# Keys and squares moved to TensorE, inversion steps in halves, and a new order of all steps in a delta-rule attention + MLP-mixer kernel

## The chip, the core and the metric

The kernel runs on one core of a Trainium2 chip. Its engines are TensorE (PE, matmuls; PEld, its weight loads), VectorE (DVE), ScalarE (ACT), GpSimd (POOL) and SyncE (SP, which issues the DMAs). The metric is device time in microseconds; the time before is 624.92 us, the median of 3 runs (623.73 to 625.54).

## The reference

```python
# q, k, v: (4, 8, 768, 48), beta: (4, 8, 768)
k_n = k / (np.linalg.norm(k, axis=-1, keepdims=True) + 1e-06)
for t in range(S):                                   # 768 steps
    y[:, :, t] = einsum('bhd,bhde->bhe', q[:, :, t], state)
    v_old = einsum('bhde,bhd->bhe', state, kt)
    state = state + bt * einsum('bhd,bhe->bhde', kt, vt - v_old)
x = y.transpose(0, 2, 1, 3).reshape(B, S, H * D)     # (4, 768, 384)
h = relu(x.T @ w_tok1) @ w_tok2                      # token mixing, 768 -> 256 -> 768
u = x + h.T
out = u + relu(u @ w_ch1) @ w_ch2                    # channel mixing, 384 -> 1536 -> 384
```

## The kernel before

The 768 steps of a batch are cut into 6 units of 128 steps, 24 units over the four batches; a unit holds two chunks of 64 steps for all 8 heads. All arithmetic is fp32. Jobs, each a Python generator, issue the work, and one long string, `order`, says how often each job is advanced and in what order. Every engine runs its own instructions in that order and waits only for what it needs; the string is thus the schedule, and nothing else sets the order. Job names are a letter and a number:

- `k` loads a unit's keys and queries, `v` its values, `w` loads and rounds a piece of a weight matrix (two ScalarE activations L286/L287, a VectorE shift L289, a GpSimd add L293).
- `p` prepares a unit (function `prep`). The squares of the keys are summed and turned into norms and scales `cs`; keys and queries are transposed by TensorE (`p_t`) and copied by ScalarE into `kq` (L566, L587); the mask times `cs` (`mb`, L574) and the keys times `cs` (L592) are made by VectorE for units 0 to 3 and by GpSimd behind them. Units 12 and up are transposed by VectorE instead.
- `c` and `d` (from unit 12 on, `c` alone) make the gram matrices of the two chunks: matmuls into `p_g` (L511), then a VectorE product with `mb` into `gm` (L517).
- `t` gathers the triangular blocks of a unit, `i` inverts those of a round of units (round 0: units 0 to 3, round 1: 4 and 5, then four at a time), `f` puts the inverse back. In rounds 0 and 1 the blocks go by copies (L674, L677, L679) into a tile `r2`, are transposed by VectorE (L731), inverted as 16x16 blocks in 14 steps of a product and an addition (L747, L751), transposed and scaled for TensorE (L757, L758, L759), and transposed back (L764). From round 2 on they go through DRAM and take 30 steps.
- `h` and `j` join the inverted blocks with matmuls (`p_z`, `p_x`, L781, L794, L855) and ScalarE copies (L785, L799, L873).
- `r` is one step of the recurrence over a chunk: `p_k` (L924), a VectorE subtraction (L931), `p_w` and `p_y` (L948, L944), a ScalarE copy (L954), `p_s` and `p_y` (L962, L963), the new state (L971). Steps r0 to r11 belong to batch 0.
- `m0` and `m1` are the mixers of batches 0 and 1; `p` L1597, `p_h` L1612 and `p_c` L1672 are their matmuls. m0 needs the steps r0 to r11. `T`, `A`, `F` and `B` are the mixers of batches 2 and 3, in forms with fewer multiplications.
- `x`, `z` and `Y` issue matmuls on zeros into a tile `p_warm` of their own; they fill idle time of TensorE.

In units 0 to 3 the keys come from the padded load by four ScalarE copies each:

```python
for cc in range(2 if u < RU else 0):
    for par in range(2):
        nc.scalar.copy(kst[PAR[par ^ cc], :, cc], heads[PAR[cc], :, par, 0:D])
```

## Time and profile before

| | |
|---|---|
| median of 3 runs | 624.92 us (623.73 to 625.54) |
| the profiled execution | 626.48 us, span 624.7 us |
| mean granted TensorE clock | 0.973 |
| busy in the span | PE 594.3 us, DVE 466.1, ACT 256.6, POOL 110.2 |

A profile is of one execution. The span runs from its first to its last instruction; its time is 1.8 us more. Busy shares are means over stages with different limits, so the stages are read one by one: the row of a window gives its start and end, its length, and the busy time and instruction count of each engine, then the granted clock of TensorE (1.00 is full), the share of the DMA engines and GB/s. A line of the timeline gives start, duration, engine, line, operation, output and input, and in brackets the idle time ahead and what ended it.

### The profile page before, as it was taken

How to read it: one execution, taken by the hardware profiler on the slowest of the kernel's cores; microseconds unless marked ns; L12 is line 12 of the kernel's file. 1: busy time of each engine (PE TensorE's matmuls, PEld its weight loads, DVE VectorE, ACT ScalarE, POOL GpSimd, SP SyncE). 2: the span in 40 equal slices, each digit the busy share in tenths (PEclk: the TensorE clock that was granted, in tenths of full speed). 3: DMA queues.
4: the chain of work that ended last, by engine and by line, in shares of the span. 5: the costliest groups of instructions: out<-in, count | busy, mean ns of one | idle time of the engine just before them, and what ended most of it. 6: DMA issues, size and time to landing. Idle time of an engine off the chain costs nothing.

```text
span 624.7 us, 20909 instructions
## 1 busy us (share of the span) xinstructions
PE 594.3 (95%) x8733; PEld 519.7 (83%) x8733; DVE 466.1 (75%) x1160; ACT 256.6 (41%) x682; POOL 110.2 (18%) x150
## 2 busy tenths in 40 slices
PE   8489898899999999999999999999999999999998
PEld 5467776667898988977888888896699999999997
DVE  4986876986889845697567986866688898675874
ACT  7748787448522344213551305423252241404200
POOL 2346355215311121003020130011000000000000
PEclk9978897999999999999999999998999999999999
DMA  9566567657653244554544443134102012020001
GB/s 220 125 140 146 143 151 192 137 139 177 129 113 71 64 103 91 102 116 96 104 74 123 93 88 76 35 80 120 32 2 39 1 17 48 14 52 13 14 26 50
DMA packets 154605, 55.52 MB, mean 89 GB/s; under 512 B 129648, under 2 KB 148976, under 8 KB 154512
## 3 DMA queue, kind: packets, MB, share of 16 engines
q1 hardware_dynamic: 154512, 54.20, 38.3%
q8 instruction: 68, 1.11, 0.8%
q14 instruction: 25, 0.20, 0.1%
HBM read 41.19 MB, written 11.21 MB: 84 GB/s over the span
## 4 chain that ended last, share of the span: by engine, by line
PE 74%; DVE 10%; DMA 4%; ACT 3%; issue 2%; SPq 2%; POOL 0%; ACTq 0%; DVEq 0%
PE p_c L1672 13%; PE p_r L1502 13%; PE p_o L1693 10%; PE p_a L1574 6%; PE p_b L1574 6%; PE p_g L511 3%; PE p_h L1612 3%; DVE x L751 2%; PE p L1597 2%; DVE sub L747 2%; PE p_k L924 1%; DMA x<-n_dram 1%; PE p_h L1242 1%; PE p_s L962 1%; PE p_y L1038 1%
## 5 line engine op out<-in xcount | busy, mean ns | idle before, releaser
L1672 PE MATMUL p_c<-u_t,wc 128*128 128x256 f32 x432 | 101.6, 386 | 0.6 <-issue 0.6
L1672 PEld LDWEIGHTS p_c<-u_t,wc 128*128 128x128 f32 x432 | 79.6, 190 | 11.9 <-issue 1.1
L1693 PE MATMUL p_o<-wc,r 128*128 128x192 f32 x360 | 64.6, 331 | 0.7 <-DVE xb L1632 0.7
L751 DVE TENSOR_TENSOR x<-x,sub 128x84 f32<-128x84 f32 (+24 forms) x178 | 59.6, 335 | 6.1
L747 DVE TENSOR_TENSOR sub<-x 128x84 f32<-128x84 f32 (+24 forms) x178 | 57.7, 324 | 8.1 <-DMA x<-n_dram 3.5
L1693 PEld LDWEIGHTS p_o<-wc,r 128*128 128x128 f32 x360 | 58.4, 190 | 2.3 <-DVE xb L1632 1.3
L1681 ACT ACTIVATE r<-p_c 128x512 f32<-128x512 f32 x36 | 21.5, 596 | 49.3 <-PE p_c L1672 43.9
L511 PE MATMUL p_g<-kq 48*64 48x128 f32 (+1 forms) x704 | 35.2, 288 | 3.0 <-ACT kq L587 3.0
L517 DVE TENSOR_TENSOR gm<-p_g,mb 128x512 f32<-128x512 f32 x44 | 28.9, 684 | 9.5 <-PE p_g L511 8.4
L484 POOL TENSOR_TENSOR v_st<-v_st,nrm 128x384 f32<-128x384 f32 x12 | 11.2, 931 | 132.4 <-DMA v_st<-in_v_dram 104.8
L511 PEld LDWEIGHTS p_g<-kq 48*64 48x64 f32 (+1 forms) x704 | 27.1, 141 | 7.9 <-ACT kq L587 4.0
L574 POOL TENSOR_TENSOR mb<-mask_c,cs 128x512 f32<-128x512 f32 x20 | 21.2, 1061 | 65.3 <-DVE cs L552 35.7
L293 POOL TENSOR_TENSOR wc<-w_f,d 128x384 uint32<-128x384 uint32 x24 | 24.6, 1030 | 43.3 <-DVE w_f L289 20.2
L1502 PE MATMUL p_r<-t_d,wc 128*128 128x192 f32 x160 | 28.8, 326 | 0.0
L1515 DVE TENSOR_TENSOR kq<-kq,p_r 128x384 f32<-128x384 f32 x40 | 21.1, 552 | 10.2 <-PE p_r L1502 8.3
L1515 DVE TENSOR_TENSOR gm<-gm,p_r 128x384 f32<-128x384 f32 x40 | 21.2, 552 | 8.1 <-PE p_r L1502 5.8
L400 DVE STREAM_TRANSPOSE kq<-pads 128x512 f32<-128x512 f32 x24 | 25.6, 1109 | 1.6 <-DMA pads<-in_k_dram 1.2
L1502 PEld LDWEIGHTS p_r<-t_d,wc 128*128 128x128 f32 x160 | 26.5, 190 | 0.0
L1693 PE MATMUL p_o<-wc,s 128*128 128x192 f32 x144 | 25.7, 330 | 0.7 <-DVE xb L1632 0.7
L1502 PE MATMUL p_r<-pads,wc 128*128 128x192 f32 x128 | 25.4, 326 | 0.0
L1693 PEld LDWEIGHTS p_o<-wc,s 128*128 128x128 f32 x144 | 23.3, 190 | 1.3 <-DVE xb L1632 1.0
L1632 DVE TENSOR_TENSOR xb<-xb,p_o 128x192 f32<-128x192 f32 x42 | 14.7, 349 | 12.7 <-PE p_o L1693 12.3
(315 smaller groups left out, 1390.6 us busy)
## 6 DMA issues: line engine op xcount, KB each, us to landing
d<-in_moe_w_ch_dram SPq DMA_DIRECT2D x24, 384.0 KB, 3.9
v_st<-in_v_dram SPq DMA_DIRECT2D x96, 48.0 KB, 2.7
out_dram<-xb SPq DMA_DIRECT2D x23, 192.0 KB, 2.1
kst<-in_k_dram SPq DMA_DIRECT2D x64, 48.0 KB, 2.6
n_dram<-gm SPq DMA_DIRECT2D x72, 32.0 KB, 2.4
pads<-in_k_dram SPq DMA_DIRECT2D x24, 96.0 KB, 3.0
pads<-in_q_dram SPq DMA_DIRECT2D x24, 96.0 KB, 2.7
gm<-w_dram SPq DMA_DIRECT2D x72, 32.0 KB, 2.1
```

The source lines that it names most:

```text
L293: nc.gpsimd.tensor_tensor(out=dst.bitcast(U32), in0=f, in1=lo, op=ALU.add)
L400: nc.vector.transpose(kq_of[p // 2][:, i, :, p % 2].rearrange("f p (s g) -> f p g s", g=G), rows_of[i].rearrange("s p (g d) -> s p g d", g ...
L511: nc.tensor.matmul(p_g[PAR[i ^ cc ^ swap(u)], p], kqt[f, p, cc, 0], kqt[f, p, cc])
L517: nc.vector.tensor_tensor(out=blocks(gm_of(u))[:, :, cc, D:GW].rearrange("s p (two n) -> s p two n", two=2), in0=p_g, in1=made[u][:, :, cc ...
L747: nc.vector.tensor_tensor(out=tmp, in0=by[0].to_broadcast(list(to.shape)), in1=by[1].to_broadcast(list(to.shape)), op=ALU.mult,)
L751: nc.vector.tensor_tensor(out=to, in0=to, in1=tmp, op=ALU.add)
L1502: nc.tensor.matmul(p[:, i], pieces[q // width][:, at : at + 128], f[f"u{n}"], start=first and i == 0, stop=True, skip_group_check=True,)
L1515: nc.vector.tensor_tensor(out=o, in0=o, in1=p, op=op_of(sign))
L1574: nc.tensor.matmul(p, a[:, i], w[:, i // 2, i % 2], start=first and i == 0, stop=True, skip_group_check=True,)
L1672: nc.tensor.matmul(p_c[:, k], piece_of(wc1, cb, f * 128)[:, f * 128 : (f + 1) * 128], u_t[:, cb], start=(cb == 0), stop=(cb == NCB - 1),)
L1681: nc.scalar.activation(r2[:, m], p_c, ACTF.Relu)
L1693: nc.tensor.matmul(p, a[:, m], wc2[:, m, j], start=(start and i == 0), stop=(i == NM - 1), skip_group_check=True,)
```

## The change

1. Squares. For units 0 to 11, `prep` now transposes the keys first, ScalarE squares the transposed keys out of PSUM, and TensorE sums the squares over the 48 features with a matmul on a column of ones, 16 for a unit, into 8 columns of `p_warm`; ScalarE takes the norms from there. The VectorE reduction is left out. The zero matmuls write 120 columns where they wrote 128.
2. Keys. For units 0 to 3, the ScalarE copies are left out; four matmuls on a piece of the identity put the keys into PSUM (`p_m`), and VectorE scales them from there.
3. Inversion. Each step's product and addition are issued in two halves (two products, then two additions), by 16x16 block in rounds 0 and 1 and by row from round 2 on.
4. The string `order` is another one.

```diff
-        nc.scalar.square(ksq, kst.rearrange("s p c d -> s (p c) d"))
-        nc.vector.tensor_reduce(out=ksum, in_=ksq, axis=mybir.AxisListType.X, op=ALU.add)
-        nc.scalar.sqrt(nrm_f, ksum)
...
+        p_t = turn(kp, True)                       # u < 12
+        yield
+        nc.scalar.square(ksq, p_t)
+        yield
+        for p in range(NP):
+            for cc in range(2):
+                for i in range(2):
+                    at = 2 * p + cc
+                    nc.tensor.matmul(
+                        p_n[PAR[i ^ cc], at : at + 1], ksq[:, p, cc], pair[:, i : i + 1]
+                    )
+        yield
+        norms(p_n, ksum)
+        yield
+        nc.scalar.copy(kqt[:, :, :, 0], p_t)
...
+        if u < RU:
+            keys = ps_seq([128, NP, 2, D], "p_m")
+            for cc in range(2):
+                for par in range(2):
+                    nc.tensor.matmul(
+                        keys[PAR[par ^ cc], :, cc], ident[:, PAR[cc]],
+                        heads[:, :, par, 0:D],
+                    )
+        scaler.tensor_tensor(out=keys_out, in0=keys, in1=wide(cs), op=ALU.mult)
...
-            nc.vector.tensor_tensor(
-                out=tmp, in0=by[0].to_broadcast(list(to.shape)),
-                in1=by[1].to_broadcast(list(to.shape)), op=ALU.mult,
-            )
-            nc.vector.tensor_tensor(out=to, in0=to, in1=tmp, op=ALU.add)
+            for to, half, by in zip(tos, tmps, bys):
+                nc.vector.tensor_tensor(
+                    out=half, in0=by[0].to_broadcast(list(to.shape)),
+                    in1=by[1].to_broadcast(list(to.shape)), op=ALU.mult,
+                )
+            for to, half in zip(tos, tmps):
+                nc.vector.tensor_tensor(out=to, in0=to, in1=half, op=ALU.add)
...
-    w10 x*4 z w10*2 z w1*4 k1*3 z k1*3 z b p1 z p1 k0*6 p0*2 b*2 p1 w2 p0*5 p1*2
+    w17 z w17*3 z x*2 w3*2 b z*3 k0*2 k1 w18 b*2 w3 k1 p1 w3 k2 p1 x p0 x*2 k3*2
```

In the changed file the lines are others: the squares' matmuls are L621, the key moves L646, the halves L814 and L819, and what was L562/L582, L511, L517, L731, L757, L758, L759, L764 is L576, L518, L524, L790, L825, L826, L827, L832.

TensorE at the first units, before. `p_t` are transposes (L562 of keys, L582 of queries), `pads` and `lent` hold the loaded rows, `p_g` grams, `p_warm` zeros:

```order
L562 MATMUL p_t<-ident,pads 128x128 x8
L582 MATMUL p_t<-ident,pads 128x128 x4
L235 MATMUL p_warm<-warm 128x512
L511 MATMUL p_g<-wc_120 64x128 x16
L582 MATMUL p_t<-ident,pads 128x128 x4
L511 MATMUL p_g<-wc_120 64x128 x16
L562 MATMUL p_t<-ident,lent 128x128 x4
L582 MATMUL p_t<-ident,lent 128x128 x4
L511 MATMUL p_g<-kq 64x128 x10
```

The same place in the changed kernel:

```order
L576 MATMUL p_t<-ident,pads 128x128 x4
L245 MATMUL p_warm<-warm 128x120
L576 MATMUL p_t<-ident,pads 128x128 x4
L245 MATMUL p_warm<-warm 128x120 x2
L621 MATMUL p_warm<-marks,ksq 64x1 x32
L576 MATMUL p_t<-ident,pads 128x128 x4
L646 MATMUL p_m<-pads,ident 64x4x48 x4
L518 MATMUL p_g<-wc_124 64x128 x16
L576 MATMUL p_t<-ident,lent 128x128 x4
L576 MATMUL p_t<-ident,pads 128x128 x4
L518 MATMUL p_g<-wc_124 64x128 x16
```

The squares of two units and one unit's key move now stand between the first transposes and the first grams.

VectorE at the end of i0, before (`x` holds the blocks, `r_124` is `r2`, `gm<-p_g` the gram products of unit 4):

```order
L751 TENSOR_TENSOR x<-x,sub 128x2x2x13
L289 TENSOR_SCALAR w_f<-d_403 128x384
L747 TENSOR_TENSOR sub<-x 128x28
L751 TENSOR_TENSOR x<-x,sub 128x2x14
L753 MEMSET x 128x32
L755 MEMSET x 128x16x16
L757 STREAM_TRANSPOSE r_124<-x 128x512
L759 TENSOR_SCALAR r_124<-r_124,even 128x512
L517 TENSOR_TENSOR gm<-p_g,mb 128x4x128 x2
L542 TENSOR_REDUCE ksum<-ksq 128x8
L764 STREAM_TRANSPOSE r_124<-x 128x1024
```

The same place in the changed kernel:

```order
L819 TENSOR_TENSOR x<-x,sub 128x2x13 x2
L524 TENSOR_TENSOR gm<-p_g,mb 128x4x128
L814 TENSOR_TENSOR sub<-x 128x14 x2
L819 TENSOR_TENSOR x<-x,sub 128x14 x2
L821 MEMSET x 128x32
L823 MEMSET x 128x16x16
L825 STREAM_TRANSPOSE r_128<-x 128x512
L827 TENSOR_SCALAR r_128<-r_128,even 128x512
L832 STREAM_TRANSPOSE r_128<-x 128x1024
L524 TENSOR_TENSOR gm<-p_g,mb 128x4x128
```

One gram product moved ahead of the last step, the other behind the back transpose, and the reduction is gone from between.

ScalarE behind i0, before (`z_571<-p_z` and `wc_120<-p_x` belong to the joins of units 0 and 1, `kq<-p_t` and `ksq` to the preparation of units 4 to 6, `d` to weights):

```order
L758 ACTIVATE r_124<-r_124,odd 128x512
L539 ACTIVATE ksq<-kst_99 128x384
L674 COPY r_124<-gm 128x8x32
L547 ACTIVATE nrm<-ksum 128x8
L548 ACTIVATE ksum<-nrm,eps 128x8
L785 ACTIVATE z_571<-p_z,sides 128x8x16 x2
L286 ACTIVATE d_609<-d_609 128x384
L287 ACTIVATE d_609<-d_609 128x384
L785 ACTIVATE z_571<-p_z,sides 128x8x16 x2
L697 ACTIVATE wc_120<-r_124,even 128x8x32 x2
L785 ACTIVATE z_571<-p_z,sides 128x8x16 x2
L566 COPY kq<-p_t 128x4x128
```

The same place in the changed kernel:

```order
L826 ACTIVATE r_128<-r_128,odd 128x512
L299 ACTIVATE d_704<-d_704 128x384
L300 ACTIVATE d_704<-d_704 128x384
L756 ACTIVATE wc_124<-r_128,even 128x8x32
L853 ACTIVATE z_712<-p_z,sides 128x8x16 x4
L756 ACTIVATE wc_124<-r_128,even 128x8x32
L853 ACTIVATE z_712<-p_z,sides 128x8x16 x2
L756 ACTIVATE gm<-r_128,even 128x8x32
L867 COPY wc_124<-p_x 16x8x16 x7
L941 COPY zst<-p_z 32x256 x2
```

The squares, norms and copies of later units no longer stand between the joins there.

318 lines of the change are left out of this document (184 added, 134 removed).

## The prediction

> **What bounds the kernel now.** I read the page first (busy shares, slices, the chain that ended last), then the windows, then the timelines of VectorE, TensorE and ScalarE ahead of 140 us.
>
> ```profile
> span 624.7 us, 20909 instructions
> PE 594.3 (95%) x8733; PEld 519.7 (83%) x8733; DVE 466.1 (75%) x1160; ACT 256.6 (41%) x682; POOL 110.2 (18%) x150
> PE   8489898899999999999999999999999999999998
> PEclk9978897999999999999999999998999999999999
> PE 74%; DVE 10%; DMA 4%; ACT 3%; issue 2%; SPq 2%; POOL 0%; ACTq 0%; DVEq 0%
> ```
>
> TensorE is the bound, except in the first eight or nine slices. The windows (length, then busy time of PE, PEld, DVE, ACT, POOL, then the granted clock) follow the program's stages: up to the first inversion (i0, 27.4 us), to its first use (h0, 41.5), to the first recurrence step (r0, 54.7), to r8 (101), to the stretch in which the mixer takes over, and the rest.
>
> ```profile
> 8.00:27.40 19.40, 14.06 (x230) 10.87 (x228) 15.24 (x38) 17.15 (x47) 4.05 (x6) 1.00 0.67 152
> 27.40:41.50 14.10, 7.67 (x44) 4.39 (x45) 12.35 (x36) 4.51 (x9) 6.45 (x6) 0.76 0.81 181
> 41.50:54.70 13.20, 12.05 (x287) 10.77 (x288) 9.13 (x16) 10.55 (x29) 7.05 (x10) 0.83 0.53 112
> 54.70:101.00 46.30, 40.71 (x1266) 36.37 (x1264) 35.21 (x92) 39.52 (x108) 25.70 (x33) 0.94 0.66 154
> 101.00:117.00 16.00, 13.50 (x237) 9.85 (x239) 11.15 (x35) 9.38 (x26) 5.53 (x7) 0.68 0.67 168
> 117.00:138.80 21.80, 21.42 (x259) 14.03 (x259) 18.46 (x54) 7.14 (x19) 4.68 (x6) 1.00 0.60 151
> 138.80:430.00 291.20, 287.11 (x5139) 246.97 (x5139) 214.32 (x549) 109.57 (x321) 52.82 (x69) 1.00 0.45 99
> 430.00:624.70 194.70, 190.80 (x1269) 182.31 (x1268) 147.36 (x327) 53.65 (x116) 0.00 (x0) 0.98 0.11 25
> ```
>
> From 117 us on TensorE is idle for 0.4 + 4.1 + 3.9 us only. What is left for it there is the same work in both programs, so faster vector steps after 117 us gain next to nothing, and the new order there has some 8 us to win or add to. The time is decided ahead of that: by when the first mixer's matmuls (m0) can run without a gap. Ahead of i0 ScalarE is the fullest (17.15 of 19.4), VectorE next; during i0 VectorE alone works (12.35 of 14.1); from 41.5 to 101 ScalarE and TensorE share the load.
>
> **Ahead of i0: keys and squares.** Prices for what goes and what comes:
>
> ```profile
> L435 ACT COPY kst<-pads x8: 337/349/352, 5.6 to 8.8; 64x192 f32<-64x192 f32 x8
> L539 ACT ACTIVATE ksq<-kst 128x384 f32<-128x384 f32 x7 | 3.7, 523 | 0.1
> L566 ACT COPY kq<-p_t 128x512 f32<-128x512 f32 x10 | 5.8, 577 | 2.4 <-PE p_t L562 2.3
> L542 DVE TENSOR_REDUCE ksum<-ksq 128x8 f32<-128x384 f32 x12 | 6.5, 545 | 4.7 <-ACT ksq L539 4.6
> 8.70 1.57 PE L257 MATMUL p_b<-pick,b_rows 32*64 32x16 f32 x48
> 10.20 1.09 PE L562 MATMUL p_t<-ident,pads 128*128 128x128 f32 x8
> 451.03 19.67 PE p_r L1502 x120
> ```
>
> Removed from ScalarE: 16 key copies at 0.35 us, 5.6 us. Its square grows from 384 to 512 elements and reads PSUM, as the kq copy does: 0.58 for 0.52, so +0.06 for each of 12 units. Removed from VectorE: 12 reductions at 0.545, 6.5 us, four or five of them ahead of i0. The scaling of units 0 to 3 by L592 now reads PSUM; masks from SBUF (L574) and gram products from PSUM (L517) cost alike there, so nothing is put down for it.
>
> Added to TensorE: the code's 24 beta matmuls are 48 records, so each fp32 matmul runs as two passes. A unit's squares are 16 matmuls, 32 passes, on 64-column weights in alternating column halves with one moving column. No row has this form. Upper end: a 128x128 transpose takes 1.09/8 = 0.136 us, half as many weight columns 0.068, so 2.2 us for a unit. Lower end: half of what the beta matmuls take, 0.5 us. Nearest is that beta row itself (64-column weights, alternating halves, short moving side): 1.57/48 = 0.033, so 1.05 us for a unit, which I take; 12.6 us for 12 units. A unit's key move is 8 passes of 192 columns at 19.67/120 = 0.164: 1.3 us one after the other, 0.65 if the two column halves overlap fully; I take 1.0, 4 us for four. In all TensorE gets 16.6 us more.
>
> The Trainium skill (TensorE: Matmul & The Clock Gate, section LDWEIGHTS) has a weight load last its columns divided by 1.2 GHz, whatever the rows: 53 ns for 64 columns. By it a unit's squares would be 32 x 53 ns = 1.7 us, an estimate, and the beta row with its 33 ns is below it; the sum would lose some 4.6 us on seven units.
>
> Of the added work, the squares of units 0 to 4 and the moves of units 0 to 2 stand ahead of unit 3's last gram: 5 x 1.05 + 3 x 1.0 = 8.3 us. In 8 to 27.4 us TensorE is idle for 5.3 us, and its fillers (two lines of code) take:
>
> ```profile
> 8.00:27.40 19.40, 2.99 (x10) 1.12 (x8) 1.00 0.67 152
> 8.00:27.40 19.40, 0.60 (x8) 0.47 (x8) 1.00 0.67 152
> ```
>
> 5.3 + 3.6 = 8.9 us, less about 0.9 for the fillers that the new order keeps there: room for 8.0. ScalarE and VectorE have slack to give now, but TensorE would be full, and it cannot be quite full: each unit's squares wait for ScalarE's square, and the next unit's grams stand behind them. If a third of its old waits stays (1.8 us), i0 begins 8.3 + 1.8 - 8.0 = **2.0 us later** (range -1 to +6). The norms also move behind the transposes, and the second unit's key lands no earlier (the same loads stand ahead of it in SP's queue, in another order).
>
> **i0 to the first recurrence step.** Within i0, starts tell what an instruction costs:
>
> ```profile
> 32.59 0.28 DVE L747 TENSOR_TENSOR sub<-x 128x112 f32<-128x112 f32 x1
> 32.90 0.28 DVE L751 TENSOR_TENSOR x<-x,sub 128x112 f32<-128x112 f32 x1
> 36.15 0.21 DVE L747 TENSOR_TENSOR sub<-x 128x52 f32<-128x52 f32 x1
> 36.39 0.21 DVE L751 TENSOR_TENSOR x<-x,sub 128x52 f32<-128x52 f32 x1
> 36.52 0.35 DVE L289 TENSOR_SCALAR w_f<-d 128x384 uint32<-128x384 uint32 x1
> 39.40 1.37 DVE L759 TENSOR_SCALAR r<-r,even 128x512 f32<-128x512 f32 x1 [0.79 <-ACT r L758]
> 40.69 1.27 DVE L517 TENSOR_TENSOR gm<-p_g,mb 128x512 f32<-128x512 f32 x2
> 116.10 0.40 DVE L751 TENSOR_TENSOR x<-x,sub 128x228 f32<-128x228 f32 x1
> 116.41 0.35 DVE L971 TENSOR_TENSOR ss_t<-ss_t,p_s 128x192 f32<-128x192 f32 x1
> 41.51 2.21 PE L781 MATMUL p_z<-r,wc 64*64 64x32 f32 x64 [2.06 <-DVE gm L517]
> ```
>
> One that needs the result ahead of it starts 0.31 us after it at 112 elements and 0.24 at 52: about 0.19 us + 1 ns an element. One that doesn't starts 0.13 after 52 elements and 0.31 after 228: about 0.08 + 1 ns. A step of N elements now takes 2 x (0.19 + N). In halves it is four instructions, each needing the one before last: two periods of max(2 x (0.08 + N/2), 0.19 + N/2), N in thousands. Over the 14 steps (28 to 112 elements, 1120 in all): 7.6 us now, 6.8 then, **-0.8 us**. Ends: -3.2 if all gaps vanish (14 x 0.23), +5.3 if an instruction always takes its full 0.19 (14 x 0.38).
>
> Against this stands a rule of the Trainium skill (VectorE: DVE Perf Modes, sections Terms and Rules for kernel authors): after every operation the pipe is flushed before the next issues, so one should minimize the count of operations. By it halves lose 5.3 us here; the L289 that started 0.13 us into a 0.21 us instruction disagrees.
>
> After the steps, the two gram products of unit 4 (40.69) stood between i0 and h0, which waited for them until 41.51. Now one is ahead of the last step and one behind the back transpose, so h0 can follow L759, 40.77 in this trace: 0.7 us earlier, less the 0.6 of the product moved ahead: **-0.1**. The back transpose itself has one product fewer ahead of it: **-0.6**, which the f jobs wait for.
>
> From there to r0 ScalarE is busy for 10.55 of 13.2 us. Two squares (0.52), two kq copies (0.58) and a copy to r2 (0.65) no longer stand between: 2.85 us. Half of it is taken, since the chain there alternates with TensorE: **-1.4 us** (0 to -2.85).
>
> ```profile
> L674 ACT COPY r<-gm 128x256 f32<-128x256 f32 x1 | 0.7, 651 | 2.2 <-DVE gm L517 2.2
> 103.12 3.94 DMA x<-n_dram
> 106.00:110.00 4.00, 4.00 (x11) 2.53 (x10) 2.96 (x13) 2.16 (x7) 0.32 (x1) 0.50 1.05 329
> ```
>
> **r0 to m0's matmuls.** From 54.7 to 101 TensorE gets four units' squares, 4.2 us, into 5.6 us of idle time; ScalarE's work is the same; VectorE loses four or five reductions and gains 0.8 us in i1, which lies on this stretch. I put **-0.4** (range -2 to +3). From 101 on, r9 to r11 run between i2's steps on VectorE (i2's input lands at 107, 103.12 + 3.94): 18 steps at 0.07 saved and two reductions are -2.3 us, against two units' squares, 2.1 us, part of them where TensorE is full: **-1.0** (range -5 to +2).
>
> Behind 138.8 us: 0, by equal work. DMAs, SP's and POOL's instructions are the same in number. In SP's queue weight loads are moved among the key and query loads; one that lands late holds ScalarE's rounding and the kq copies behind it, which is the upper end of i0's range.
>
> **Sum:** 2.0 - 0.8 - 0.1 - 0.6 - 1.4 - 0.4 - 1.0 = **-2.3 us**: a span of 622.4, and 624.2 for this execution, whose own time was 626.5 beside a span of 624.7. Its time lies 1.6 above the median of the runs, 624.92; against that median I predict **622.6 us**.
>
> **Rivals.**
> - The cold stretch goes too. At 106 to 110 the clock was 0.50, after TensorE's waits of 101 to 106, and in 101 to 117 it idled for 2.5 us. With more to do there and i2 begun ahead of r8, it may stay warm: 2.5 idle + about 2 of slowed matmuls back, 618. Against it: TensorE still follows VectorE there.
> - No difference. The relief of ScalarE and VectorE ahead of i0 is worth nothing, since TensorE, full by then, sets i0's start, and r8 onwards follows i2, which waits for DMA round trips as before. Then the -1.4 and -1.0 go, i0's delay is cancelled by the rest: 625.
> - Slower: the squares cost 0.068 a pass, 2.2 us a unit. That is 1.15 more for each: 5.7 ahead of i0 and 2.3 on the last two units, 630.6. It decides from 2.3 / 7 = 0.33 us a unit more, that is 0.043 a pass; the transposes speak for it, the beta row against.
> - Slower: every half pays in full. At 0.19 us + 1 ns an element whatever it depends on, a step costs 0.38 us more: 5.3 in i0, as much in i1, 6.8 in i2's 18 steps, half of it on the chain, and the 2.3 saved in steps lost: 633.5. The two starts inside running instructions speak against it. It is what the rule of the Trainium skill (VectorE: DVE Perf Modes, section Terms) would bring.
>
> **How the numbers follow.** Chances: the forecast 0.33 (its own range 619.5 to 623), the warm stretch 0.13, no difference 0.26, costly squares 0.19, flush 0.04, a new wait elsewhere in the new order 0.05. A measurement of this kernel tells about 0.3% (1.9 us) from no change. Faster by more than that: 0.13 + 0.32 = 0.45; same: 0.26; slower: 0.29, from the last three and a sliver of the forecast. The range, 613 to 632, reaches past the warm stretch and over the costly squares.
>
> **What would show it.** The new matmuls' rows: 1.05 us a unit for the squares, 1.0 for a move. i0's transpose (L731 before) at 29.4 instead of 27.4, with TensorE over 95% busy ahead of it. Its 14 steps in 6.8 us, halves starting inside each other. r0 near 53.8, r8 near 99, the first p_c near 136.5, TensorE's idle time behind it still about 8 us. I am wrong if a unit's squares take over 1.4 us, if i0 starts beyond 32, or if idle time of several us appears behind 140 us.

## The result, and the profile after

The changed kernel takes 663.72 us (median of 4 runs, 660.36 to 670.45), the kernel before 624.33 us (median of 4, 623.58 to 625.54): a ratio of 1.0611, 95% interval 1.0557 to 1.0665. In the run of 670.45 us the chip was in a slower state, and the ratios leave such runs out. The prediction was 622.6 us. The profiled execution took 660.36 us beside a span of 658.6; the spans below are compared with the 624.7 of before.

From the page of the changed kernel, the span and the busy times:

```profile
span 658.6 us, 22031 instructions
PE 614.6 (93%) x9149; PEld 532.5 (81%) x9149; DVE 466.9 (71%) x1497; ACT 252.2 (38%) x666; POOL 109.6 (17%) x150
```

TensorE is busy for 20.3 us more than the 594.3 of before, and idle for 13.6 us more. Where, three windows tell: up to the first p_c, from there to the first matmul of the third mixer, and the rest (columns as above). First before:

```profile
0.00:138.70 138.70, 116.27 (x2330) 90.36 (x2330) 104.44 (x284) 93.32 (x247) 57.26 (x82) 0.90 0.67 156
138.70:422.00 283.30, 279.71 (x4987) 242.11 (x4983) 210.05 (x542) 105.80 (x307) 51.32 (x68) 1.00 0.44 96
422.00:624.70 202.70, 198.30 (x1425) 187.24 (x1421) 151.64 (x335) 57.52 (x131) 1.60 (x1) 0.98 0.14 33
```

and the same windows of the changed kernel:

```profile
0.00:161.20 161.20, 137.41 (x2795) 105.89 (x2795) 100.46 (x392) 90.23 (x232) 59.51 (x83) 0.89 0.63 134
161.20:459.90 298.70, 282.39 (x4968) 242.54 (x4966) 214.68 (x771) 104.16 (x303) 47.16 (x64) 0.99 0.43 93
459.90:658.60 198.70, 194.78 (x1397) 184.06 (x1389) 151.78 (x335) 57.85 (x132) 2.96 (x3) 1.00 0.14 32
```

Two different losses. Ahead of the first p_c 22.5 us: TensorE is busy 21.1 us longer, and its idle time has not shrunk (22.4 us, now 23.8), although ScalarE and VectorE have 3 and 4 us less to do. Behind it 15.4 us, 12.7 of them idle time (3.6 us, now 16.3). The last window gives 4.0 back; its granted clock was 0.98 in the execution before.

The larger part of the first loss lies behind i0. From r1's p_w to the first p_c, before:

```profile
59.50:138.70 79.20, 70.73 (x1632) 55.49 (x1630) 62.59 (x174) 51.80 (x141) 32.35 (x41) 0.91 0.62 153
```

and now:

```profile
66.40:161.20 94.80, 84.32 (x1893) 66.20 (x1891) 63.36 (x259) 54.63 (x142) 34.57 (x41) 0.87 0.57 129
```

15.6 us more, 13.6 of them busy time of TensorE, at a lower clock.

The new matmuls, from the groups by line (count, busy time, mean ns of one, idle time ahead):

```profile
L621 PE MATMUL p_warm<-marks,ksq 128*64 128x1 f32 x384 | 14.0, 202 | 2.3 <-ACT ksq L614 2.3
L646 PE MATMUL p_m<-lent,ident 128*64 128x192 f32 x16 | 1.7, 339 | 0.0
```

The moves out of `pads` take another 1.7 us. 14.0 / 12 = 1.17 us for a unit's squares (0.036 us a pass) and 3.4 / 4 = 0.85 for a move: 17.4 us in all, about the 16.6 put down. The price of the matmuls themselves was right; what was wrong is what their place in the schedule costs.

The first two units on TensorE and ScalarE, from the timeline of the changed kernel:

```profile
10.10 0.66 PE L576 MATMUL p_t<-ident,pads 128*128 128x128 f32 x4
10.79 0.60 ACT L614 ACTIVATE ksq<-p_t 128x512 f32<-128x512 f32 x1
11.78 1.10 PE L621 MATMUL p_warm<-marks,ksq 128*64 128x1 f32 x32
12.99 0.60 ACT L614 ACTIVATE ksq<-p_t 128x512 f32<-128x512 f32 x1 [1.61 <-PE p_warm L621]
13.64 1.10 PE L621 MATMUL p_warm<-marks,ksq 128*64 128x1 f32 x32 [0.77 <-ACT ksq L614]
...
16.32 1.59 PE L518 MATMUL p_g<-wc 64*64 64x128 f32 x32 [0.19 <-ACT wc L638]
...
18.76 0.54 ACT L299 ACTIVATE d<-d 128x384 f32<-128x384 f32 x1 [1.61 <-DMA d<-in_moe_w_ch_dram]
20.29 0.56 ACT L638 COPY wc<-p_t 128x512 f32<-128x512 f32 x1
20.90 1.15 PE L518 MATMUL p_g<-wc 64*64 64x128 f32 x32 [1.97 <-ACT wc L638]
```

The first grams of the kernel before:

```profile
12.60 1.37 PE L511 MATMUL p_g<-wc 64*64 64x128 f32 x32
15.94 1.16 PE L511 MATMUL p_g<-wc 64*64 64x128 f32 x32 [1.38 <-ACT wc L587]
```

Before, ScalarE squared the loaded keys of units 0 and 1 and VectorE summed them at 7 to 10.3 us, while TensorE ran zeros and the beta matmuls; nothing of it stood behind a transpose. Now the transposes come first, at the same 10.1 us, and behind them TensorE and ScalarE take turns: square, sums, next square (it waits until the sums have read `ksq`), sums, norms, copies, grams. The first grams start 3.7 us later. The second ones start 5.0 later, and a weight load has a part in this: ScalarE waited 1.6 us for it at 18.76 and rounded the weights ahead of the copy that these grams need. i0 starts at 35.9 in place of 27.4.

VectorE in i0. A line holds both halves of a step's product (x2); the additions between them are left out:

```profile
38.64 0.32 DVE L814 TENSOR_TENSOR sub<-x 128x44 f32<-128x44 f32 x2
39.12 0.33 DVE L814 TENSOR_TENSOR sub<-x 128x50 f32<-128x50 f32 x2
...
41.90 0.36 DVE L302 TENSOR_SCALAR w_f<-d 128x384 uint32<-128x384 uint32 x1 [1.19 <-ACT d L299]
```

A step of 88 elements in halves takes 39.12 - 38.64 = 0.48 us; the formula of the prediction gives 0.50. But a weight's rounding now stands inside the steps and waits for ScalarE, 1.2 us in which VectorE does nothing.

Behind the first p_c, what TensorE waited for (in all, times, longest), in the changed kernel:

```profile
PE p_k L992 <- DVE ss_t L1039: 3.6, 3, 3.2
PE p_o L1761 <- DVE xb L1700: 2.8, 3, 1.1
PE p_k L1081 <- DVE ss_t L1138: 2.0, 1, 2.0
PE p_z L923 <- DVE t L885: 2.0, 2, 1.0
```

and in the same stretch before, where the longest wait was 0.7:

```profile
PE p_o L1693 <- DVE xb L1632: 1.4, 3, 0.7
```

All of them are waits for VectorE, most for its steps of the recurrence and the joins. The longest, 3.2 us at 265 us, shows what stood in front there. A later unit's keys land late; ScalarE's square waits for them, VectorE's sum waits for the square, and the state (L1039) that TensorE needs stands behind the sum.

```profile
266.89 0.52 ACT L584 ACTIVATE ksq<-kst 128x384 f32<-128x384 f32 x1 [4.61 <-DMA kst<-in_k_dram]
267.44 0.55 DVE L587 TENSOR_REDUCE ksum<-ksq 128x8 f32<-128x384 f32 x1 [4.71 <-ACT ksq L584]
...
268.27 0.32 DVE L1039 TENSOR_TENSOR ss_t<-ss_t,p_s 128x192 f32<-128x192 f32 x1
```

Other waits of this stretch lead back to loads in the same way. Two waits of a join at 351 us (1.2 us together) are for a gram product that stands behind such a sum, three of joins at 239, 324 and 458 us (2.4 together) for a VectorE transpose that waits for its blocks from DRAM, and the 2.0 us of L1081 end behind an inversion whose blocks VectorE had waited 5.2 us for. That is 8.8 of the 16.3 us of idle time. ScalarE's squares waited 29.1 us in all for keys here, and 7.5 before.

### The profile page after: what moved, and what is told of

The parts are those of the page before. It is cut to its first block, busy times and chain, and to the rows that moved or that the text cites. A ratio compares the mean times of both kernels' runs of the same rounds, so it can differ in the third digit from the quotient of the medians.

```text
span 658.6 us, 22031 instructions
## 1 busy us (share of the span) xinstructions
PE 614.6 (93%) x9149; PEld 532.5 (81%) x9149; DVE 466.9 (71%) x1497; ACT 252.2 (38%) x666; POOL 109.6 (17%) x150
## 5 line engine op out<-in xcount | busy, mean ns | idle before, releaser
L1740 PE MATMUL p_c<-u_t,wc 128*128 128x256 f32 x432 | 103.6, 389 | 1.1 <-issue 0.9
L814 DVE TENSOR_TENSOR sub<-x 128x56 f32<-128x56 f32 (+41 forms) x351 | 73.1, 248 | 10.8 <-DMA x<-n_dram 8.8
L819 DVE TENSOR_TENSOR x<-x,sub 128x56 f32<-128x56 f32 (+41 forms) x351 | 71.0, 242 | 0.2
L518 PE MATMUL p_g<-kq 48*64 48x128 f32 (+1 forms) x704 | 35.7, 280 | 8.9 <-ACT kq L638 7.3
L518 PEld LDWEIGHTS p_g<-kq 48*64 48x64 f32 (+1 forms) x704 | 26.9, 136 | 14.3 <-ACT kq L638 8.5
L524 DVE TENSOR_TENSOR gm<-p_g,mb 128x512 f32<-128x512 f32 x44 | 29.0, 683 | 10.8 <-PE p_g L518 10.7
L1761 PE MATMUL p_o<-wc,s 128*128 128x192 f32 x144 | 25.8, 331 | 0.8 <-DVE xb L1700 0.8
L1580 ACT COPY kq<-p_r 128x384 f32<-128x384 f32 x24 | 11.4, 476 | 37.8 <-PE p_r L1570 35.8
L299 ACT ACTIVATE d<-d 128x384 f32<-128x384 f32 (+1 forms) x34 | 18.4, 540 | 17.4 <-DMA d<-in_moe_w_ch_dram 9.0
```

What stands on the lines that cost most here:

```text
L518: nc.tensor.matmul(p_g[PAR[i ^ cc ^ swap(u)], p], kqt[f, p, cc, 0], kqt[f, p, cc])
L524: nc.vector.tensor_tensor(out=blocks(gm_of(u))[:, :, cc, D:GW].rearrange("s p (two n) -> s p two n", two=2), in0=p_g, in1=made[u][:, :, cc ...
L814: nc.vector.tensor_tensor(out=half, in0=by[0].to_broadcast(list(to.shape)), in1=by[1].to_broadcast(list(to.shape)), op=ALU.mult,)
L819: nc.vector.tensor_tensor(out=to, in0=to, in1=half, op=ALU.add)
L1740: nc.tensor.matmul(p_c[:, k], piece_of(wc1, cb, f * 128)[:, f * 128 : (f + 1) * 128], u_t[:, cb], start=(cb == 0), stop=(cb == NCB - 1),)
L1761: nc.tensor.matmul(p, a[:, m], wc2[:, m, j], start=(start and i == 0), stop=(i == NM - 1), skip_group_check=True,)
```

## The experiments

Times are medians; a ratio is to the kernel before on the same chip, with its 95% interval. The rows were measured on several chips, so that small differences are to be read from the ratios. "Old order" is the order of before. Where the code has other steps than that order, a unit's steps stand at its old places, as each expectation says. The expectations also name the theories between which a run is to decide.

| kernel | us | ratio |
|---|---|---|
| halves, old order | 619.53 | 0.9921 (0.9893 to 0.9950) |
| halves in rounds 0 and 1 alone, old order | 619.76 | 0.9969 (0.9931 to 1.0006) |
| halves, three more zero matmuls, old order | 623.32 | 0.9992 (0.9958 to 1.0025) |
| halves + key moves, old order | 622.79 | 0.9972 (0.9937 to 1.0007) |
| halves + key moves, squares of units 0 to 3 (2 of 16 matmuls), old order | 628.96 | 1.0081 (1.0045 to 1.0118) |
| halves + key moves, squares of units 0 to 3, old order | 634.16 | 1.0174 (1.0104 to 1.0243) |
| halves + squares of units 4 to 11 (2 of 16 matmuls), old order | 636.33 | 1.0202 (1.0139 to 1.0266) |
| halves + squares of units 4 to 11, old order | 642.35 | 1.0266 (1.0212 to 1.0320) |
| the same and a zero matmul a unit | 646.53 | 1.0348 (1.0280 to 1.0415) |
| the same, squares out of SBUF | 653.29 | 1.0494 (1.0431 to 1.0557) |
| all edits, old order | 655.85 | 1.0510 (1.0455 to 1.0564) |
| all edits, new order: the changed kernel | 663.72 | 1.0611 (1.0557 to 1.0665) |

The parts add up: halves -0.8%, moves and squares of units 0 to 3 +2.5%, squares of units 4 to 11 +3.5%, together 1.052; all edits in the old order measured 1.051. The new order adds some 1.0% to that; the two intervals just touch, and the traces under experiment 3 tell more.

**1. Halves alone.**

```diff
 # kernel before, inversion steps
-nc.vector.tensor_tensor(out=tmp, ...); nc.vector.tensor_tensor(out=to, ...)
+two products, then two additions, as in the change
```

> The kernel before with one part of the change, the steps of the inversions in two halves; the order and everything else as before. Theory work (the 17.4 us that TensorE is busy longer, 14.0 for squares and 3.4 for key moves, lie on its path wherever they stand): the halves cost nothing, the two early rounds gain about 28 x 0.13 = 3.6 us on VectorE, of which some reaches the end: 620 to 625. Theory order (what is lost is lost to waits of the new order): the same, 620 to 625. Theory halves (twice as many VectorE instructions delay whatever VectorE does between them): 630 or more, with TensorE idle behind 140 us.

619.53 us, 0.9921: a gain of 0.8%, 4.9 us. Theory halves is out. The halves are the one part of the change that pays. Their gain is more than the 2.9 us of the prediction (0.8 in i0, as much in i1, 1.3 in i2).

**2. The changed kernel with whole steps.**

```diff
-            for to, half, by in zip(tos, tmps, bys): ...
+            nc.vector.tensor_tensor(out=tmp, ...); nc.vector.tensor_tensor(out=to, ...)
```

> The changed kernel with the steps of the inversions whole again; squares, key moves and the new order stay. Theories work and order: 663 to 668, since the halves are worth a few us at most. Theory halves: 650 or less, the 13.5 us of TensorE's additional idle time are gone.

664.21 us, 1.0645 (1.0570 to 1.0720). The loss is not the halves'; in the new order their gain does not stand out from the noise.

**3. All edits in the old order.**

```diff
 # order of before
-k0*6 p0*2 b*2 p1 w2 p0*5 p1*2
+k0*2 p0*2 b*2 p1 w2 p0*5 p1*2     # no key copies; p0 to p3 have one step more near their end
```

> The changed kernel's squares, key moves and halves in the order of before. A unit's steps stand at the places where its old steps stood: for units 0 and 1 one for one, for the others transposes and square at the place of the old fourth step, the squares' matmuls at the fifth, norms and copy at the sixth, scales and mask at the seventh; the key move beside the last step or the one before it. Theory work: 17.4 us less what the halves gain and what fits into idle time, 634 to 642. Theory order: 621 to 629, since the additional waits belong to the new order and the early stage has idle time and zero matmuls enough. Below 625 would say that all the loss is the order's.

655.85 us, 1.0510: above what either theory gave. Its windows:

```profile
0.00:171.40 171.40, 147.41 (x2747) 115.25 (x2747) 101.21 (x389) 90.01 (x231) 57.35 (x82) 0.81 0.59 127
171.40:455.10 283.70, 279.52 (x4986) 242.17 (x4982) 214.38 (x776) 106.62 (x310) 51.42 (x68) 1.00 0.44 97
```

The second window, behind the first p_c, is 283.7 us with 4.2 idle, as before: the 15 us there belong to the new order alone. The other traces bear this out. From the first p_c to the start of the last one it is 260.0 to 263.3 us in all thirteen profiled kernels with the old order, and 275.6 to 279.7 in all seven with the new one. Ahead of the first p_c the old order is worse, 171.4 against 161.2, with a granted clock of 0.81. So the new order comes to the first p_c 10 us earlier, and loses more than that behind it. And the edits cost 36 us beside the halves alone, not 17: something more than the matmuls' own time is lost.

**4. Two of sixteen square matmuls, new order.**

```diff
-for p ...: for cc ...: for i ...:
-    nc.tensor.matmul(p_n[PAR[i ^ cc], at : at + 1], ksq[:, p, cc], pair[:, i : i + 1])
+for i in range(2):
+    nc.tensor.matmul(p_n[PAR[i]], ksq[:, 0, 0], pair[:, i : i + 1].to_broadcast([128, NB]))
```

> The changed kernel in its own order with 2 of a unit's 16 square matmuls left, each writing eight columns: the norms come from the sums of one block alone, all other work is as in the changed kernel. It takes 24 x 14/16 and more, some 12 us, off TensorE. Theory work: 650 to 654, the whole 12 us come back. Theory order: 660 or more, since TensorE then waits longer at the same places.

659.60 us, 1.0552 (1.0484 to 1.0620): 4 of the 12 us, and the interval overlaps with that of the changed kernel. i0 stays at 35.8, but not because the sums cost nothing. Unit 0's grams start at 14.03 us, 2.3 earlier than in the changed kernel; then ScalarE waits for the weight load of above, which lands no earlier, and unit 1's grams stand behind it as late as there (the copy L638 is L633 here):

```profile
18.81 0.54 ACT L299 ACTIVATE d<-d 128x384 f32<-128x384 f32 x1 [3.94 <-DMA d<-in_moe_w_ch_dram]
20.96 2.04 PE L518 MATMUL p_g<-wc 64*64 64x128 f32 x32 [4.31 <-ACT wc L633]
```

Behind it the clock was at one half for 7 us of this execution, and at full in the one of the changed kernel. So this run cannot tell what the sums cost in i0; experiment 15 can, in the old order.

**5. Later units' squares, old order.**

```diff
+OLD_SQ = (0, 1, 2, 3)      # prepared as before, with ScalarE's key copies
+# units 4 to 11: squares on TensorE; old places 4: transposes, square; 5: sums; 6: norms, copy; 7: scales, mask
```

> The order of before with the halves and with the squares of units 4 to 11 summed by TensorE; units 0 to 3 are prepared as before, with ScalarE's key copies. Theory chain (the loss ahead of i0 is the longer way to the norms of units 0 to 3: transposes, square, sums, norms one behind the other; the later units' squares are nearly free): 617 to 623, beside 619.5 for the halves alone. Theory later units (each later unit's squares and its longer hold on a PSUM bank delay the joins and the recurrence, 14 us from r0 to m0): 630 to 636.

642.35 us, 1.0266: 23 us above the halves alone, for 8 x 1.17 = 9.4 us of matmuls. The stretch from r1's p_w to the first p_c, first with the halves alone:

```profile
57.80:135.90 78.10, 69.56 (x1629) 54.60 (x1629) 64.02 (x260) 52.25 (x142) 32.58 (x41) 0.93 0.65 158
```

and here:

```profile
62.50:163.50 101.00, 88.51 (x1824) 71.61 (x1818) 61.09 (x254) 53.09 (x141) 32.08 (x40) 0.78 0.51 120
```

TensorE is busy 19.0 us longer, of which 8.6 are squares, and idle for 4.0 more. The rest goes with the clock column, 0.78 against 0.93: the same 192 passes of the grams take 14.9 us in place of 12.1, the 24 passes of m0's first matmul (L1606, here L1718) 11.5 in place of 9.8. (This execution took 646.75 us, the longest of the four.)

**6. Key moves alone, old order.**

```diff
+keys = ps_seq(...)            # first step: four matmuls on pieces of the identity
+nc.scalar.square(ksq, keys)   # out of PSUM; VectorE sums as before
```

> The order of before with the halves and with the keys of units 0 to 3 moved by TensorE, as a unit's first step; ScalarE squares them out of PSUM, VectorE sums them as before, no square goes to TensorE. Theory chain: the way to the norms loses a ScalarE copy and gains a TensorE step that stands behind the zero matmuls and the beta matmuls: 616 to 622, i0 at 26 to 28 us. Theory work (TensorE's busy time lies on the path): 3.4 us of key moves above 619.5, 622 to 625.

622.79 us, 0.9972: 0.5% above the halves alone, in the range of theory work, but the two intervals overlap. i0's transpose (first of its two starts) in the kernel with halves alone:

```profile
L731 DVE STREAM_TRANSPOSE x<-r x2: 1234/1240/1245, 27.0 to 61.0; 128x1024 f32<-128x1024 f32 x2
```

and with the moves:

```profile
L843 DVE STREAM_TRANSPOSE x<-r x2: 1235/1240/1246, 30.2 to 62.8; 128x1024 f32<-128x1024 f32 x2
```

3.2 us for 3.4 us of moves, although 5.6 us of ScalarE copies are gone. (In the eight profiled kernels with the halves that prepare units 0 to 3 as before, i0 starts between 27.0 and 28.3 us, so such differences are good to about 1 us.)

**7. Units 0 to 3 as before, in the new order.**

```diff
+OLD_SQ = (0, 1, 2, 3); the four key copies stand right behind k0 to k3's loads
```

> The changed kernel in its new order, but units 0 to 3 prepared as before (key copies on ScalarE, squares from the keys, VectorE's sums, the old sequence of steps at the new places); units 4 to 11 keep their squares on TensorE. Theory chain: i0 at 28 to 31 us in place of 35.9, 654 to 659. Theory order: i0 at 34 or later, 661 or more. Theory later units: 654 or more, with the 6 to 14 us from r0 to the first p_c still lost.

679.64 us, 1.0887. This one tells nothing on the question: in the new order the next units' loads stand ahead of the old scaling and write the same `kst`, so that the scaling waits for them and reads their rows.

**8. The copy ahead of the sums, new order.**

```diff
         nc.scalar.square(ksq, p_t)
+        nc.scalar.copy(kqt[:, :, :, 0], p_t)
...
-        nc.scalar.copy(kqt[:, :, :, 0], p_t)   # behind the norms
```

> The changed kernel with one instruction moved: ScalarE's copy of the transposed keys into kq stands right behind the square, ahead of the sums and norms, so that the PSUM bank of the transposes comes free some 2 us earlier for each unit. Theory later units (the bank): 650 to 657, most of it between r0 and the first p_c. Theories chain and order: 659 to 664, nothing but a few tenths at i0.

662.11 us, 1.0608 (1.0546 to 1.0671): no change; in the new order the bank's hold is not what costs. (Some units' keys are overwritten here ahead of their last use.)

**9. Two of sixteen, later units, old order.** The edit of experiment 4 in experiment 5's kernel.

> The order of before with halves and TensorE's squares for units 4 to 11 (642.4 us with all 16 matmuls of a unit), now with 2 of the 16 matmuls, each writing eight columns: the norms of those units come from one block's sums alone. Theory clock (the granted clock was at one half for 65 us of that kernel, 24 us in the one without these squares, and stood low where the squares stand; matmuls of one moving column don't hold it up): half-clock time back to 25 to 35 us, 622 to 628. Theory bank (the transposes hold their PSUM bank over square, sums, norms and copy, and the joins wait): 636 or more. Theory work (9.4 us of matmuls on the path, at whatever clock): 631 to 635.

636.33 us, 1.0202 (1.0139 to 1.0266): 6 us back, at theory bank's bound, though the interval overlaps with that of experiment 5. The same stretch:

```profile
59.10:150.20 91.10, 78.19 (x1657) 61.04 (x1650) 61.74 (x255) 53.18 (x142) 32.37 (x41) 0.83 0.60 140
```

9.9 of the 22.9 us are gone; 14/16 x 8.6 = 7.5 us is the price of the matmuls left out. Thirteen stay, with a clock of 0.83.

**10. A wide zero matmul behind each unit's squares.**

```diff
+        nc.tensor.matmul(p_warm[:, 0 : 4 * ZW]..., zero, zero[:, None, 0:ZW].to_broadcast([128, 4, ZW]))
```

> The same kernel with all 16 matmuls, and behind each unit's 16 one more zero matmul of 480 columns into the fillers' columns: about 0.67 us a unit, 5.4 us of TensorE work more. Theory clock: the wide matmuls count as activity, the half-clock stretches between 50 and 107 us shrink, and the kernel gets faster although it does more: 630 to 639 against 642.4. Theories work and bank: slower, 645 to 648.

646.53 us, 1.0348 (1.0280 to 1.0415): 4 us slower, with overlapping intervals. The clock of the stretch rose to 0.83 from 0.78. But the zeros took TensorE 10.6 us by the trace, not the 5.4 put down, and ScalarE's norms waited for them seven times, 14.0 us in all: they lengthen the way to the norms. What the higher clock is worth is therefore not shown.

**11. Weights behind unit 1's query copy, new order.**

```diff
-w10*2 k4 d0 w10*2 d0*2 k4 p1 p2 w1*2 w2 p1*2 d1*2
+k4 d0*3 k4 p1 p2 p1*2 w10*4 w1*2 w2 d1*2
```

> The changed kernel with one edit of its order: seven steps of weight pieces (loads, rounding on ScalarE, VectorE and GpSimd), which stood ahead of unit 1's query copy, stand behind it. In the changed kernel ScalarE waited 1.6 us for a weight load at 18.8 us and rounded for 1.5 us more, and unit 1's grams waited 2.2 us for the copy behind them. Theory order (that wait is part of what i0 loses): unit 1's first gram near 18 in place of 20.9 us, i0 at 33 to 34.5, 660 to 662. Theory chain (i0 follows the alternation of TensorE and ScalarE over four units, whatever stands between): the grams come earlier, i0 stays above 35, 662 to 665.

665.32 us, 1.0667 (1.0615 to 1.0719), and i0 at 38.2: above 35, as theory chain had it. But the rounding was moved and not removed: it now stands ahead of unit 2's square, and the sums of that unit wait 1.8 us for the square. The clock was also at one half for some 3 us from 14.2 and again from 24.5 in this execution, and at full in the changed kernel's. What the wait for the weight load is worth stays open.

**12. Zeros against the cold stretch, with halves, old order.**

```diff
-h5 r8*3 w29 t8*3 w29 w27*2 r8*2 w29*2 q3 ... r8*3 p9
+h5 r8*3 w29 t8*3 w29 z w27*2 r8*2 w29*2 z q3 ... r8*2 z r8 p9
```

> The kernel before with the halves (619.5 us) and three zero matmuls of 512 columns more, at 97 to 105 us, where TensorE waits for 0.5 to 1.4 us at a time and the clock was at one half from 100 to 107 us. Theory clock: the half-clock stretch there goes, up to 3 us of slowed matmuls come back for 1.6 us of zeros, most of these in waits: 617 to 620. If zeros of this size don't hold the clock: 619.5 to 621.

623.32 us, 0.9992 (0.9958 to 1.0025): slower than without. The half-clock stretch of 7 us at 100 us did go, but another of 7 us came at 113, and the zeros, 3.4 us by the trace, brought nothing back.

**13. Squares out of SBUF, later units, old order.**

```diff
+        nc.scalar.copy(kqt[:, :, :, 0], p_t)        # at its old place
+        nc.scalar.square(ksq, kqt[:, :, :, 0])      # then sums, norms, one or two places later
```

> The order of before with halves and all 16 square matmuls for units 4 to 11, as in the kernel of 642.4 us, but the transposes and the copy into kq stand where they stood before, and ScalarE squares that copy out of SBUF: the PSUM bank of the transposes is held no longer than before, and the square waits for nothing. Sums and norms stand one or two places later. Theory bank (of the 23 us over the halves alone, some 14 that were left with 2 of 16 matmuls come from the bank held longer and from ScalarE's waits in front of square and norms): 626 to 631. Theory work and clock (the matmuls alone): 631 to 636. Theory way (the norms wait for TensorE, wherever the copy stands): 638 or more.

653.29 us, 1.0494 (1.0431 to 1.0557): 11 us slower again. What theory bank forecast did not come; theory way's range did. The stretch:

```profile
62.20:173.90 111.70, 93.37 (x1827) 75.96 (x1823) 61.51 (x255) 54.69 (x142) 32.22 (x41) 0.74 0.49 111
```

TensorE is idle for 18.3 us of it, against 8.5 with the halves alone. Most of that is one wait: the sums' matmuls stand on TensorE before ScalarE has made the squares. Here, and in experiment 5 (in all, times, longest):

```profile
PE p_warm L676 <- ACT ksq L669: 11.6, 6, 5.8
PE p_warm L674 <- ACT ksq L667: 2.1, 3, 0.7
```

So the round trip from TensorE to ScalarE and back stops TensorE itself, and does so the longer, the later ScalarE comes to the square. Since sums and norms also stand later here, what the bank's hold costs by itself in the old order is not measured.

**14. Units 0 to 3 in the changed way, old order.**

```diff
+OLD_SQ = units 4 to 11; units 0 to 3: key moves and squares on TensorE
```

> The order of before with halves; units 0 to 3 alone are prepared in the changed way (squares and key moves on TensorE), units 4 to 11 as before. With the squares left to VectorE the key moves put i0 at 30.2 us and the end at 622.8; all edits in the order of before put i0 at 39.7. Theory chain (the way transposes, square, sums, norms of the first units, one after the other, sets i0): i0 at 38 to 41, and what i0 loses reaches the end: 629 to 634. Theory cover (the later stages have slack for it): i0 as late, but below 627.

634.16 us, 1.0174. i0:

```profile
L843 DVE STREAM_TRANSPOSE x<-r x2: 1237/1241/1245, 39.9 to 72.1; 128x1024 f32<-128x1024 f32 x2
```

12.9 us later than with the halves alone, and 15 us at the end: no cover behind it.

**15. Two of sixteen in that kernel.** The edit of experiment 4.

> The order of before with halves and units 0 to 3 prepared in the changed way (634.2 us, i0 at 39.9 us), now with 2 of a unit's 16 square matmuls: the norms of those four units come from one block's sums alone. The four units' matmuls were 4.7 us of the 12.8 by which i0 was late. Theory work: i0 at 35 to 36, 629 to 631. Theory chain (transposes, square, sums, norms and copies alternate between TensorE and ScalarE, and how long the sums take matters little): i0 at 38 or later, 631 to 635, as the changed kernel with the same cut kept its i0 at 35.8 us.

628.96 us, 1.0081. i0:

```profile
L838 DVE STREAM_TRANSPOSE x<-r x2: 1236/1241/1246, 34.9 to 66.9; 128x1024 f32<-128x1024 f32 x2
```

Here theory work is right about this term: 14 of 16 matmuls are 4.1 us, and i0 comes 5.0 earlier. The 12.9 us are thus some 3 for the moves, some 5 for the sums' matmuls and, as what is left, some 5 for the longer way, each to about 1 us.

**16. Later square and sum for units 12 to 23, new order.** In the order, the first two steps of `p12` to `p23` stand right ahead of the third.

> The changed kernel with one edit of its order: for units 12 to 23, which ScalarE and VectorE square and sum as before, the square and the sum stand right ahead of the norms in place of one to some steps earlier. ScalarE waited 29 us in all for these units' keys in the changed kernel, and a VectorE sum stood in front of a state that TensorE waited 3.2 us for, at 265 us. Theory late keys (the waits behind the first p_c come from VectorE and ScalarE standing in front of keys that land late): 3 to 8 of the 15 us behind the first p_c come back, 655 to 660. Theory scattered order (many small waits of different kinds): 660 to 664.

667.92 us, 1.0701 (1.0630 to 1.0772). Nothing comes back. But the edit did not take the wait away; the same square still waits for its keys, VectorE's sum behind it, and TensorE for 3.6 us:

```profile
271.84 0.52 ACT L584 ACTIVATE ksq<-kst 128x384 f32<-128x384 f32 x1 [5.00 <-DMA kst<-in_k_dram]
```

ScalarE's squares still waited 19.6 us for keys behind the first p_c, and VectorE's transposes 9.9 for blocks from DRAM, against 5.1 in the changed kernel. So theory late keys is neither shown nor refuted by this run. A run with the new order that issues these loads as early as before would tell; there is none.

**17. Halves in rounds 0 and 1 alone.**

> The kernel before with halves in the two early rounds alone, where VectorE works by itself while TensorE waits. Halves in all rounds gave 619.5 us, 5 less than before. If the gain is the early rounds' (i0 to h0 1 us shorter, passed on to the end): 620 to 623. If the later rounds give it (30 steps at 0.05 us, four rounds, beside a full TensorE): 623 to 625.

619.76 us, 0.9969 (0.9931 to 1.0006). The interval reaches from the full gain of the halves to none; how the gain divides over the rounds stays open.

**18. One-column matmuls by themselves.**

```diff
+wide()                                   # 20 zero matmuls of 512 columns
+for n in range(400):
+    nc.tensor.matmul(p_tail[PAR[n % 2], 0, at : at + 1], ident[:, 0:C], ident[:, 0:1])
+wide()
```

> The kernel before with halves, and behind its last matmul three blocks that nothing waits for: 20 zero matmuls of 512 columns, then 400 matmuls of the squares' form (64 weight columns, one moving column, 800 passes, at 0.036 us some 29 us), then 20 of 512 columns again. What matters is the granted clock in the middle block. Theory clock (one-column matmuls don't count as enough activity): it falls to one half within about 10 us of that block, and the third block's first matmuls take twice the time of the first block's. Theory waits (the clock falls only where TensorE really waits, and the half-clock stretches of the other kernels come from their waits): it stays at 1.00 through all three blocks.

One execution, span 693.2 us. The three blocks, from the timeline:

```profile
615.47 17.33 PE L1869 MATMUL p_tail<-warm 128*128 128x512 f32 x40
632.73 39.40 PE L1874 MATMUL p_tail<-ident 128*64 128x1 f32 x800
672.06 20.30 PE L1869 MATMUL p_tail<-warm 128*128 128x512 f32 x40
```

and windows through the middle block and the third:

```profile
634.00:635.00 1.00, 1.00 (x41) 1.00 (x39) 0.00 (x0) 0.00 (x0) 0.00 (x0) 1.00 0.00 0
635.00:640.00 5.00, 5.00 (x130) 5.00 (x128) 0.00 (x0) 0.00 (x0) 0.00 (x0) 0.69 0.01 3
650.00:655.00 5.00, 5.00 (x98) 5.00 (x98) 0.00 (x0) 0.00 (x0) 0.00 (x0) 0.50 0.02 3
675.00:680.00 5.00, 5.00 (x9) 2.08 (x9) 0.00 (x0) 0.00 (x0) 0.00 (x0) 0.71 0.00 0
```

TensorE is busy for the whole of every row, and the clock falls to one half about 4 us after the first one-column matmul (0.69 over 635 to 640 is 3.1 us at one half), stays there, and comes back some 6 us after the wide ones begin (0.71 over 675 to 680). The third block takes 3.0 us more than the first for the same matmuls. Theory clock is shown for this form of matmul. How much of the changed kernel's time it is no run tells, and the clock differs from one execution to the next: three of them had clocks of 0.971, 0.969 and 0.961 and spans of 658.6, 660.4 and 663.4 us.

## Why the prediction was wrong, step by step

- **Ahead of i0, "8.3 us of work into room 8.0": wrong.** 2.0 us were predicted, 8.5 measured. The work was sized well: 9.4 us of squares and moves in 8 to 35.9 us. The room was not there. It was the sum of TensorE's idle time and its zeros, and neither came free: 2.6 us of zeros stayed in the new order where 0.9 were put, and 4.5 us of idle time where 1.8 were put. The idle time is waits for ScalarE's copies at fixed places, which the new work does not fill but lengthens, since it needs ScalarE ahead of it and has ScalarE behind it. The old squares of units 0 and 1, by contrast, stood under cover: their key copies run at 5.6 to 9.2 us, squares and sums up to 10.3, and the first transposes start at 10.2. To take them from there won nothing that i0 shows. Experiments 6, 14 and 15 give the shares for the old order. In the new order the late weight load has a share too, which the prediction had named as the upper end of its range (experiments 4 and 11); how large it is stays open.
- **i0's steps, -0.8 us: right in size.** Without the foreign work inside (the rounding with its wait, one gram product, one late addition) the 14 steps take 6.8 us, as predicted. From i0 to r0 the time went from 27.1 to 25.8 us (r0's first matmul at 54.5, now 61.7): 1.3 us shorter, 2.9 were predicted. Nearly all of it came behind h0's first matmul (49.9 us, before 41.5), where 1.4 were put; up to there only 0.1 was won, and the 1.2 us wait of the rounding stands in that part. What was too small is the worth of the halves in all: 4.9 us alone (experiment 1), against 2.9 for i0, i1 and i2 together. The rival in which every half pays in full is out, and with it, for this kernel, the Trainium skill's counsel to minimize the count of operations (VectorE: DVE Perf Modes, section Rules for kernel authors): the measurement decides.
- **r0 to m0's p_c, -0.4 and -1.0 us: wrong.** From r1's p_w on this stretch lost 15.6 us. The same kind of room was filled here ("4.2 us, into 5.6 us of idle time"): idle time went from 8.5 to 10.5, and busy time up by 13.6, of which 6.3 are squares and 1.7 more zeros. Some of the rest is work that the new order puts into this stretch (208 passes of the grams for 192, 192 of p_z L923 for 130 of its L855 before). What remains goes with a price that the sum had no term for, a lower granted clock (0.87 for 0.91; in the old order, where the matmuls are the same but for the squares, 0.78 for 0.93). Nor had it a term for TensorE's waits in front of the sums, 11.6 us in experiment 13.
- **Behind the first p_c, 0 "by equal work": wrong.** Equal work in a new order lost 15.4 us there, 12.7 of them idle, in 14 waits of over 0.3 us. The prediction gave the order "8 us to win or add to" and then put 0; a new wait in the new order was a rival at 0.05 and deserved far more, because a stretch with 1.3% idle time (3.6 of 283.3 us) has little to win and much to lose. That the order is the cause is shown (experiment 3). In the one trace that was followed, 8.8 of the 16.3 idle us lead back to loads that land late for this order; that they are the cause is not tested by a run (experiment 16).
- **The sum's own alarms** were right: i0 beyond 32 us and idle time behind 140 us were named as signs of error. The rival of costly squares had the right sign for the wrong reason: 0.036 us a pass, far below its 0.068. By the Trainium skill (TensorE: Matmul & The Clock Gate, section LDWEIGHTS) it would have been 53 ns; the measurement decides here too. In experiment 18 a pass of this form took 51 ns at half the clock and 24 ns at full.
- What stays open: the thirteen microseconds that are left between r1's p_w and the first p_c with 2 of 16 matmuls (experiment 9), where the clock was still 0.83, are split between the way and the clock by no run.

## What to carry to other kernels

Idle time of a full engine is not room: before work is moved into it, name the wait that makes the gap, and whether the new work ends that wait or stands in it. Work that was done early on idle engines cost this kernel little; moved to the engine that everything waits for, behind a round trip with another engine, it cost more than its own time (i0 12.9 us later for 8.1 us of matmuls in four units, experiment 14). A new order over a stretch with 1.3% idle time has little to win and is a risk to be priced: ask of each load whether it still lands before the engine comes to it. Of several edits in one change each is to be tried alone: here the halves by themselves, in the order of before, are the best version measured, 0.9921.

## What the hardware showed

One-column matmuls, one directly after the other, do not hold TensorE's clock: with TensorE busy all the time, it fell to 0.50, and a pass went from 1.00 / 41 = 0.024 to 5.00 / 98 = 0.051 us. The Trainium skill (TensorE: Matmul & The Clock Gate, section Part 1: The HAM clock gate) has the clock follow how busy the array was in a window of about 3.4 us; the way down took some 4 us here and the way back some 6, which agrees with one to two such windows. But busy in the sense of the trace is not what the gate sees: by the trace's busy time the rule would have kept the clock at full. So a granted clock below 1.00 beside a full TensorE can come from thin matmuls, without any wait.

Zeros against a cold clock did not make the kernel faster in either place tried, although the clock rose: with 3.4 us of them it took 3.8 us more (experiment 12), with 10.6 us some 4 more (experiment 10, where the intervals overlap and ScalarE's norms waited for the zeros).
